# Unordered scatters, contiguous normalised rows and woven routing in an attention-then-experts kernel

## The chip, the cores and the metric

The kernel runs on one core of a Trainium2 chip. The metric is the device time of one execution in microseconds (us). The kernel before takes 444.11 us (median of 2 runs, 443.06 to 445.15). Ratios below are the mean time of one kernel's fast runs over that of the other's of the same rounds, so they are not quite the ratio of the medians that are quoted.

## The reference

```python
# attention with pooled keys and values: 8 batches, 8 heads, 576 queries, 64 per head
k_p = k.reshape(B, H, 72, 8, D).mean(axis=3);  v_p = likewise
attn = softmax(q @ k_p.T / 8)
x = (attn @ v_p)                      # 4608 rows of 512
# each row goes to one of 8 experts, by its domain id
for e in range(8):
    out[dom == e] = relu(x[dom == e] @ w1[e]) @ w2[e]     # 512 -> 1024 -> 512
```

## The kernel before

The kernel has three stages. Set-up loads the inputs and works out the routing: for every row its rank within its expert, hence its slot, and the inverse (for every slot its row). Attention runs in four pairs of batches. Each pair makes nine tiles of 128 normalised rows, and each tile is scattered to its slots in a DRAM buffer, `x_slots`. The expert stage reads the slots of an expert back, transposed, multiplies twice, and scatters the output rows to `out`. The first 384 slots of expert 0 are worked on inside pair 3.

```python
def load_pair(t_ap, pr, tag):                    # all loads are issued from GpSimd, and cast to F16
    t = io.tile([128, 72, D], F16, tag=tag, bufs=2, name=tag)
    nc.gpsimd.dma_start(t[:]..., t_ap[2 * pr:2 * pr + 2]...)

# normalise a tile of rows (half the heads at a time), then scatter it
if qd == 0:
    s["x", cc] = wk.tile([128, HD], F16, tag="x_sb", bufs=8, name="x_sb")
nc.vector.reciprocal(rcp[:], pv[:, :, 64])
xo = x_sb[:].rearrange("p (b h a) -> p h a b", b=4, h=H)[:, 4 * qd:4 * qd + 4]
nc.vector.tensor_tensor(out=xo, in0=pv[:, :, 0:64].rearrange("p h (a b) -> p h a b", b=4),
                        in1=rcp[:]...to_broadcast([128, 4, 16, 4]), op=ALU.mult)
if qd == 1:
    nc.gpsimd.indirect_dma_start(out=x_slots[:], out_offset=...(ap=slot_i[:, c:c + 1], axis=0), in_=x_sb[:], ...)

def xload(e, s0, s1):                            # slots back to the chip, transposed by the DMA
    xT = late.tile([128, 4, CAP], F16, tag="xT", bufs=2, name="xT")
    nc.sync.dma_start_transpose(xT[:, :, 0:s1 - s0], x_slots[CAP * e + s0:CAP * e + s1, :])

# second expert layer, a block of 128 slots
y = late.tile([128, HD], F32, tag="y", bufs=4, name="y")
nc.gpsimd.indirect_dma_start(out=out, out_offset=...(ap=orig[:, bl:bl + 1], axis=0), in_=y[:], ...)

# order of the program (cut)
...                                               # routing, about 100 small VectorE operations
for pr in range(NP):                              # the inverse of the slots
    perm_build(pr); perm_mm(pr)
perm_finish()
run(kp_units(0)); run(vp_units(0))                # pool k and v of pair 0
for pr in range(NP):
    run(qt_units(pr))
    if pr + 2 < NP: kt[pr + 2] = load_pair(k, ...); vt[pr + 2] = load_pair(v, ...)
    if pr == 3:
        for e in range(2):
            xload(e, 0, EARLY)
            if e > 0: wload(e)
    fill = kp_units(pr + 1) + vp_units(pr + 1)    # or, in pair 3, expert_units(0, 0, EARLY)
    run(merge(scav_units(pr), fill, ...))
    if pr + 2 < NP: qt_[pr + 2] = load_pair(q, ...)
    if pr == 0: wload(0)
wload(2)
...                                               # per task: xload of the next one, units, wload(e + 3)
```

The softmax here doesn't subtract the row's maximum and nothing guards it: scores larger than these inputs give would overflow.

Of the kernel before, what the change touches and what calls it, by code (L numbers as in the profile page):

```python
# [36 lines left out]
def kernel(  # L37
# [19 lines left out]

    def big():
        return ps.tile([128, 2, 512], F32, tag="big", bufs=2, name="big")
# [7 lines left out]
    x_slots = dram.tile([XROWS, HD], F16, name="x_slots")  # L67

# [7 lines left out]
    with tc.manual_schedule():  # L76
# [7 lines left out]
        nc.scalar.dma_start(  # L84
            x_slots[0:E * CAP, :].rearrange("(e s) d -> e (s d)", e=E)[:, FILL * HD:CAP * HD]
            .rearrange("e (p c) -> p e c", p=128),
            zt[:].unsqueeze(1).to_broadcast([128, E, 4 * (CAP - FILL)]))
# [16 lines left out]
        qt_[0] = load_pair(q, 0, "q")  # L104
        kt[1] = load_pair(k, 1, "k")
# [36 lines left out]
        for cc in range(NC_):  # L142
# [3 lines left out]
            if cc >= 4:  # L146
# [21 lines left out]
        rk = small()  # L168
        nc.tensor.matmul(rk[:, 0:8 * (NCH + 1)], Ls[:], oh[:].rearrange("p c e -> p (c e)"),
                         start=True, stop=False)  # L170
        for c in range(NCH - 1):
            c1 = NCH + 1 if c < EPAIR * NC_ else NCH
            nc.tensor.matmul(rk[:, 8 * (c + 1):8 * c1].rearrange("p (c e) -> p c e", e=E), ones[:],
                             oh[:, c, :].unsqueeze(1).to_broadcast([128, c1 - c - 1, E]),
                             start=False, stop=(c == NCH - 2))
        rkv = rk[:, 0:8 * NCH].rearrange("p (c e) -> p c e", e=E)

        gap = rt.tile([128, E], F32, name="gap")
        nc.vector.memzero(gap[:])
        nc.vector.tensor_scalar(out=gap[:, 0:NEARLY], in0=rk[:, 8 * NCH:8 * NCH + NEARLY],  # L180
                                scalar1=-1.0, scalar2=float(EARLY), op0=ALU.mult, op1=ALU.add)
        nc.vector.tensor_scalar(out=gap[:, 0:NEARLY], in0=gap[:, 0:NEARLY], scalar1=0.0,
                                scalar2=None, op0=ALU.max)
        tmp = rt.tile([128, NCH, E], F32, name="tmp")
        c0 = EPAIR * NC_
        nc.vector.tensor_copy(tmp[:, 0:c0], rkv[:, 0:c0])
        nc.vector.tensor_tensor(tmp[:, c0:NCH], rkv[:, c0:NCH],
                                gap[:].unsqueeze(1).to_broadcast([128, NCH - c0, E]), op=ALU.add)
        nc.vector.tensor_tensor(tmp[:], tmp[:], oh[:, 0:NCH, :], op=ALU.mult)
        rank = const.tile([128, NCH], F32, name="rank")  # L190
        nc.vector.tensor_reduce(out=rank[:], in_=tmp[:], op=ALU.add, axis=AX.X)
        ovf = const.tile([128, NCH], F32, name="ovf")
        nc.vector.tensor_scalar(out=ovf[:], in0=rank[:], scalar1=float(CAP), scalar2=None,
                                op0=ALU.is_ge)
        slotf = rt.tile([128, NCH], F32, name="slotf")
        nc.vector.tensor_scalar(out=slotf[:], in0=dom[:], scalar1=float(CAP), scalar2=None,
                                op0=ALU.mult)
        nc.vector.tensor_tensor(slotf[:], slotf[:], rank[:], op=ALU.add)

        ovf_h = rt.tile([128, NCH], F16, name="ovf_h")  # L200
        nc.vector.tensor_copy(ovf_h[:], ovf[:])
        ork = small()
        nc.tensor.matmul(ork[:, 0:NCH], Ls[:], ovf_h[:], start=True, stop=False)
        for c in range(NCH - 1):
            nc.tensor.matmul(ork[:, c + 1:NCH], ones[:],
                             ovf_h[:, c:c + 1].to_broadcast([128, NCH - 1 - c]),
                             start=False, stop=(c == NCH - 2))

        od = rt.tile([128, NCH], F32, name="od")
        nc.vector.tensor_scalar(out=od[:], in0=ork[:, 0:NCH], scalar1=float(NBLK * 128),  # L210
                                scalar2=None, op0=ALU.add)
        nc.vector.tensor_tensor(od[:], od[:], slotf[:], op=ALU.subtract)
        nc.vector.tensor_tensor(od[:], od[:], ovf[:], op=ALU.mult)
        nc.vector.tensor_tensor(od[:], od[:], slotf[:], op=ALU.add)
        slot_i = const.tile([128, NCH], I32, name="slot_i")
        nc.vector.tensor_copy(slot_i[:], od[:])

        nov = rt.tile([128, 2], F16, name="nov")
        ovs = rt.tile([128, 1], F32, name="ovs")
        nc.vector.tensor_reduce(out=ovs[:], in_=ovf[:], op=ALU.add, axis=AX.X)  # L220
        nc.vector.tensor_copy(nov[:, 0:1], ovs[:])
        nc.vector.tensor_copy(nov[:, 1:2], ovs[:])
        novp = small()
        nc.tensor.matmul(novp[:, 0:2], ones[:], nov[:], start=True, stop=True)
        nov_f = const.tile([128, 1], F32, name="nov_f")
        nc.vector.tensor_copy(nov_f[:], novp[:, 0:1])
        nblk_f = const.tile([128, 1], F32, name="nblk_f")
        nc.vector.tensor_scalar(out=nblk_f[:], in0=nov_f[:], scalar1=127.0, scalar2=None, op0=ALU.add)
        nblk_i = const.tile([128, 1], I32, name="nblk_i")
        nc.vector.tensor_copy(nblk_i[:], nblk_f[:])  # L230
        nc.vector.tensor_scalar(out=nblk_i[:], in0=nblk_i[:], scalar1=7, scalar2=None,
                                op0=ALU.logical_shift_right)

        mrow = const.tile([128, NCH], I32, name="mrow")
        mt = rt.tile([128, NCH], F32, name="mt")
        nc.vector.tensor_scalar(out=mt[:], in0=ovf[:], scalar1=-float(BIG), scalar2=float(BIG - NBLK * 128),
                                op0=ALU.mult, op1=ALU.add)
        nc.vector.tensor_tensor(mt[:], mt[:], od[:], op=ALU.add)
        nc.vector.tensor_copy(mrow[:], mt[:])


        pos_i = rt.tile([128, NCH], I32, name="pos_i")
        nc.vector.tensor_scalar(out=pos_i[:], in0=slot_i[:], scalar1=127, scalar2=None,
                                op0=ALU.bitwise_and)
        blk_i = rt.tile([128, NCH], I32, name="blk_i")
        nc.vector.tensor_scalar(out=blk_i[:], in0=slot_i[:], scalar1=7, scalar2=None,
                                op0=ALU.logical_shift_right)
        pos_h = const.tile([128, NCH], F16, name="pos_h")
        nc.vector.tensor_copy(pos_h[:], pos_i[:])
        blk_h = const.tile([128, NCH], F16, name="blk_h")  # L250
        nc.vector.tensor_copy(blk_h[:], blk_i[:])

        m_i = rt.tile([128, NC_], I32, name="m_i")
        nc.vector.tensor_scalar(out=m_i[:], in0=n_i[:], scalar1=3, scalar2=None,
                                op0=ALU.logical_shift_right)
        m_f = rt.tile([128, NC_], F32, name="m_f")
        nc.vector.tensor_copy(m_f[:], m_i[:])
        tk = rt.tile([128, NC_], F32, name="tk")
        nc.vector.tensor_scalar(out=tk[:], in0=m_f[:], scalar1=2.0, scalar2=None, op0=ALU.mult)
        t1 = rt.tile([128, NC_], F32, name="t1")  # L260
        for thr, add in ((36, -71.0), (72, 503.0), (108, -71.0)):
            nc.vector.tensor_scalar(out=t1[:], in0=m_f[:], scalar1=float(thr), scalar2=add,
                                    op0=ALU.is_ge, op1=ALU.mult)
            nc.vector.tensor_tensor(tk[:], tk[:], t1[:], op=ALU.add)
        g72 = rt.tile([128, 1], F32, name="g72")
        nc.vector.tensor_scalar(out=g72[:], in0=g_f[:], scalar1=72.0, scalar2=None, op0=ALU.mult)
        nc.vector.tensor_scalar(out=tk[:], in0=tk[:], scalar1=g72[:, 0:1], scalar2=None, op0=ALU.add)
        tok = rt.tile([128, NP, NC_], F32, name="tok")
        nc.vector.tensor_tensor(tok[:], pr_i[:], tk[:].unsqueeze(1).to_broadcast([128, NP, NC_]),
                                op=ALU.add)  # L270
        tok_i = rt.tile([128, NCH], I32, name="tok_i")
        nc.vector.tensor_copy(tok_i[:], tok[:].rearrange("p a c -> p (a c)"))
        th_i = rt.tile([128, NCH], I32, name="th_i")
        nc.vector.tensor_scalar(out=th_i[:], in0=tok_i[:], scalar1=6, scalar2=None,
                                op0=ALU.logical_shift_right)
# [53 lines left out]
        for pr in range(NP):  # L329
            perm_build(pr)  # L330
            perm_mm(pr)
# [216 lines left out]
        def run(units):  # L548
            for f in units:
                f()  # L550
# [143 lines left out]
```

## Time and profile before

| | before |
|---|---|
| time, median | 444.11 us |
| span of the profiled execution | 440.8 us |
| TensorE, VectorE busy | 59%, 39% |
| mean granted TensorE clock | 0.756 of full |

No engine is full. The first part of the page gives the busy time of each engine. In its table of groups a line gives the source line, engine, operation, output and inputs, shapes and count, then the busy time and the mean length of one in ns, then the engine's idle time just before them and what ended most of it.

```profile
span 440.8 us, 5605 instructions
...
PE 260.2 (59%) x2328; PEld 181.3 (41%) x2328; DVE 172.6 (39%) x321; ACT 94.2 (21%) x153; POOL 94.1 (21%) x113
...
L442 DVE TENSOR_TENSOR x_sb<-small,rcp 128x256 f16<-128x256 f32 x72 | 93.5, 1299 | 22.9 <-DMA x_slots<-x_sb,slot_i 19.3
...
L539 POOL DMA_INDIRECT out_dram<-y,orig x40 | 39.8, 995 | 149.1 <-DMA out_dram<-y,orig 117.5
L447 POOL DMA_INDIRECT x_slots<-x_sb,slot_i x36 | 35.6, 990 | 144.2 <-DVE rcp L439 63.7
...
```

Two things stand out. The multiply on line 442 takes 1299 ns for 256 columns. The two scatters on GpSimd are short to issue (about 1 us), but GpSimd is idle for some 145 us before each kind, and for the output scatter what ends that idle time is mostly the landing of another output scatter.

The windows view gives, for stretches of the span, the busy time of each engine, the granted clock, the share of the DMA engines that was busy, and GB/s. The stretches here start at the first scores of pairs 0, 1, 2 and 3 (50.0, 81.2, 128.8, 163.3), at the first expert matmul (192.0), after the last row scatter (235) and after the last matmul (415.7).

```profile
...
core 0: us, PE busy (x) PEld busy (x) DVE busy (x) ACT busy (x) POOL busy (x), PEclk, DMA share, GB/s
50.00:81.20 31.20, 23.46 (x344) 17.46 (x344) 26.55 (x43) 14.47 (x23) 6.77 (x7) 0.74 0.30 73
81.20:128.80 47.60, 24.76 (x346) 18.50 (x346) 26.61 (x43) 14.40 (x23) 8.97 (x13) 0.61 0.64 139
128.80:163.30 34.50, 23.53 (x344) 17.34 (x344) 26.58 (x43) 14.59 (x23) 9.43 (x10) 0.70 0.28 70
163.30:192.00 28.70, 0.69 (x4) 0.21 (x4) 0.00 (x0) 1.18 (x2) 6.07 (x7) 0.50 0.55 118
192.00:235.00 43.00, 34.34 (x216) 19.58 (x217) 29.50 (x47) 13.51 (x24) 12.10 (x13) 0.85 0.14 47
235.00:415.70 180.70, 132.57 (x726) 89.64 (x723) 34.90 (x50) 29.80 (x49) 40.31 (x46) 0.85 0.62 138
415.70:440.80 25.10, 0.36 (x2) 0.00 (x0) 0.00 (x0) 0.60 (x1) 3.29 (x4) 0.59 0.11 40
...
```

Pair 3 takes 71.7 us, of which 28.7 is TensorE doing nothing. The experts take 180.7 us with TensorE busy for 132.57.

GpSimd's timeline shows how the row scatters are released:

```profile
...
91.70 1.03 POOL L447 DMA_INDIRECT x_slots<-x_sb,slot_i  x1 [1.18 <-DVE x_sb L442]
119.16 1.02 POOL L447 DMA_INDIRECT x_slots<-x_sb,slot_i  x1 [26.42 <-DMA x_slots<-x_sb,slot_i]
122.39 0.98 POOL L447 DMA_INDIRECT x_slots<-x_sb,slot_i  x1 [2.22 <-DMA x_slots<-x_sb,slot_i]
...
```

The scatter at 119.16 waited 26.42 us: its predecessor was issued at 91.70 and landed 26.7 us later, at 118.4, after the loads that stood before it in the queue (the last of them, v of the next pair, issued at 89.94, took 28.1 us and landed at 118.0). The next one comes 3.23 us later: one issue of 1.02 us and one landing (2.5 us). In the waits view (engine and line, what it waited for, us in total, times, longest) this reads:

```profile
...
POOL out_dram L539 <- DMA out_dram<-y,orig: 117.5, 25, 12.8
...
POOL x_slots L447 <- DMA x_slots<-x_sb,slot_i: 47.1, 9, 26.4
...
PE big L514 <- DMA xT<-x_slots: 42.0, 2, 28.0
...
DVE y L535 <- DMA out_dram<-y,orig: 26.2, 2, 15.5
...
DVE x_sb L442 <- DMA x_slots<-x_sb,slot_i: 19.3, 2, 16.2
...
```

### The profile page before, as it was taken

What the parts mean: (1) busy time and instruction counts of PE and PEld (TensorE: products, weight loads), DVE (VectorE), ACT (ScalarE), POOL (GpSimd) and SP (SyncE); (2) the same over time, 40 slices, a digit from 0 to 9 for tenths busy, and PEclk for the clock granted to TensorE, in tenths of its full rate; (3) what the DMA queues carried; (4) which work ended last, traced back from release to release, by engine and by line L of the source; (5) the groups of instructions that cost most, each with busy time, mean ns of one, the idle gap of its engine ahead of it and who ended that gap; (6) DMA issues with size and microseconds to landing.
All of it is one profiled execution on the core that took longest, in us unless ns stands there. A gap on an engine that the chain in (4) does not pass through costs nothing. (4 is left out here: it accounts for less than half of the span.)

```text
span 440.8 us, 5605 instructions
## 1 busy us (share of the span) xinstructions
PE 260.2 (59%) x2328; PEld 181.3 (41%) x2328; DVE 172.6 (39%) x321; ACT 94.2 (21%) x153; POOL 94.1 (21%) x113
## 2 busy tenths in 40 slices
PE   2317795792079360057594299909849597499700
PEld 2216574481057240025251268506426364268300
DVE  4585399692269670019770032203203022033100
ACT  1000742731055330025111023101111110113100
POOL 5000012330022232101243030202212132122220
PEclk9756887586557855559888599967959979599955
DMA  8997921199611611850117859962936829211110
GB/s 200 227 215 151 183 58 37 37 197 217 137 37 39 131 37 48 165 109 12 61 59 155 179 128 195 219 146 79 209 103 146 185 80 214 86 69 73 62 67 0
DMA packets 30909, 52.34 MB, mean 119 GB/s; under 512 B 22750, under 2 KB 23838, under 8 KB 27296
## 3 DMA queue, kind: packets, MB, share of 16 engines
q0 software_dynamic: 8960, 45.10, 44.0%
q1 hardware_dynamic: 20880, 5.28, 6.6%
q10 hardware_dynamic: 1040, 1.57, 1.2%
q8 instruction: 19, 0.31, 0.3%
q14 instruction: 10, 0.08, 0.1%
HBM read 61.90 MB, written 16.78 MB: 179 GB/s over the span
## 5 line engine op out<-in xcount | busy, mean ns | idle before, releaser
L514 PE MATMUL big<-xT,w 128*128 128x320 f16 (+2 forms) x512 | 89.4, 337 | 78.1 <-DMA xT<-x_slots 42.0
L514 PEld LDWEIGHTS <-w 128*128 128x128 f16 x512 | 71.9, 149 | 94.1 <-issue 67.0
L442 DVE TENSOR_TENSOR x_sb<-small,rcp 128x256 f16<-128x256 f32 x72 | 93.5, 1299 | 22.9 <-DMA x_slots<-x_sb,slot_i 19.3
L520 DVE TENSOR_SCALAR hT<-big 128x640 f16<-128x640 f32 (+2 forms) x40 | 28.4, 711 | 122.8 <-PE big L514 120.9
L530 PE MATMUL small<-w,hT 128*128 128x512 f16 x320 | 72.8, 386 | 0.3 <-DVE y L535 0.3
L539 POOL DMA_INDIRECT out_dram<-y,orig x40 | 39.8, 995 | 149.1 <-DMA out_dram<-y,orig 117.5
L447 POOL DMA_INDIRECT x_slots<-x_sb,slot_i x36 | 35.6, 990 | 144.2 <-DVE rcp L439 63.7
L518 ACT ACTIVATE hT<-big 128x640 f16<-128x640 f32 (+2 forms) x40 | 23.9, 597 | 119.0 <-PE big L514 90.4
L530 PEld LDWEIGHTS <-hT 128*128 128x128 f16 x320 | 31.6, 99 | 36.8 <-issue 2.3
L416 ACT ACTIVATE at<-big 72x576 f16<-72x576 f32 x64 | 40.0, 644 | 27.9 <-PE big L413 26.8
L435 PE MATMUL small<-vp,at 72*128 72x65 f16 (+1 forms) x320 | 24.0, 214 | 31.0 <-DVE rcp L439 27.4
L535 DVE COPY y<-small 128x512 f32<-128x512 f32 x20 | 14.0, 702 | 63.8 <-PE small L530 37.7
L435 PEld LDWEIGHTS <-at 72*128 72x128 f16 (+1 forms) x320 | 16.1, 110 | 42.7 <-issue 24.7
L413 PE MATMUL big<-qT,kpT 64*72 64x288 f16 x128 | 24.2, 379 | 10.2 <-DVE hT L520 4.1
L537 ACT ACTIVATE y<-small 128x512 f32<-128x512 f32 x20 | 12.0, 598 | 81.1 <-PE small L530 50.1
L439 DVE RECIPROCAL rcp<-small 128x4 f32<-128x4 f32 x72 | 23.3, 324 | 10.5 <-PE small L435 10.5
L351 PE MATMUL small<-ident,k 128*64 128x128 f16 x576 | 23.1, 253 | 0.6 <-DVE x_sb L442 0.6
L351 PEld LDWEIGHTS <-k 128*64 128x64 f16 x576 | 21.5, 133 | 2.0 <-DVE x_sb L442 0.8
L399 PE MATMUL small<-ident,q 128*128 128x128 f16 x144 | 15.8, 286 | 2.6 <-DVE rcp L439 1.6
L413 PEld LDWEIGHTS <-kpT 64*72 64x72 f16 x128 | 8.9, 121 | 18.4 <-issue 12.0
L374 ACT ACTIVATE vT<-small 128x512 f16<-128x512 f32 (+1 forms) x12 | 5.8, 489 | 46.7 <-PE small L372 46.7
L399 PEld LDWEIGHTS <-q 128*128 128x128 f16 x144 | 13.2, 132 | 4.4 <-issue 2.6
(114 smaller groups left out, 126.4 us busy)
## 6 DMA issues: line engine op xcount, KB each, us to landing
w<-in_moe_w_dram POOLq DMA_DIRECT2D x16, 1024.0 KB, 12.6
k<-in_k_dram POOLq DMA_DIRECT2D x4, 1152.0 KB, 17.6
v<-in_v_dram POOLq DMA_DIRECT2D x4, 1152.0 KB, 22.9
q<-in_q_dram POOLq DMA_DIRECT2D x4, 1152.0 KB, 14.8
x_slots<-zt ACTq DMA_DIRECT2D x1, 1536.0 KB, 19.3
out_dram<-y,orig POOLq DMA_INDIRECT x40, 2.8
x_slots<-x_sb,slot_i POOLq DMA_INDIRECT x36, 2.4
xT<-x_slots SPq DMA_TRANSPOSE x10, 8.2
```

Source lines behind the costliest of these rows:

```text
L351: nc.tensor.matmul(pv[64 * half:64 * half + 64, w, :], kk[:, 8 * (w0 + w) + t, :], ident[:], start=(t == 0), stop=(t == 7), skip_group_che ...
L399: nc.tensor.transpose(p[:, j, :], qq[:, 128 * (j0 + j):128 * (j0 + j) + 128], ident[:])
L413: nc.tensor.matmul(p[0:72, par, 0:288], s["kpT"][64 * par:64 * par + 64, bh, :], s["qT"][64 * par:64 * par + 64, :, 8 * bh:8 * bh + 8], st ...
L416: nc.scalar.activation(at[0:72, bh % 8, :].rearrange("p (a c) -> p a c", a=2), p[0:72, :, 0:288], AFT.Exp, scale=1.0 / 64.0)
L435: nc.tensor.matmul(pv[r0:r0 + z - a, hh, :], s["at", bt][0:72, h, a:z], s["vp"][0:72, 8 * bt + h, :], start=True, stop=True, skip_group_ch ...
L442: nc.vector.tensor_tensor(out=xo, in0=pv[:, :, 0:64].rearrange("p h (a b) -> p h a b", b=4), in1=rcp[:].unsqueeze(2).unsqueeze(3).to_broad ...
L447: nc.gpsimd.indirect_dma_start(out=x_slots[:], out_offset=bass.IndirectOffsetOnAxis(ap=slot_i[:, c:c + 1], axis=0), in_=x_sb[:], in_offset ...
L514: nc.tensor.matmul(p[:, a, 0:m], w1[:, kk, fi:FF:8], xT[:, kk, m * a:m * a + m], start=(kk == 0), stop=(kk == 3))
L518: nc.scalar.activation(dst, p[:, 0:nh, 0:m], AFT.Relu)
L520: nc.vector.tensor_scalar(out=dst, in0=p[:, 0:nh, 0:m], scalar1=0.0, scalar2=None, op0=ALU.max)
L530: nc.tensor.matmul(p[:], hT[:, fi, 128 * j:128 * j + 128], w2[:, fi, :], start=(fi == 0), stop=(fi == 7))
L539: nc.gpsimd.indirect_dma_start(out=out, out_offset=bass.IndirectOffsetOnAxis(ap=orig[:, bl:bl + 1], axis=0), in_=y[:], in_offset=None, bou ...
```

## The change

The change has three intents. (a) Scatters no longer wait for one another, since every row has its own destination; the transposed read still waits for all of them. (b) The normalising multiply walks its output in the order in which it lies in SBUF. (c) Only rank and slot stay ahead of the scores of pair 0; everything else of the routing is spread over pairs 0 to 2. With these come two small moves: the zero fill of `x_slots` goes behind the first loads, and the evictions of pair 0's pooled keys go to ScalarE. The diff is cut to its core and a little simplified.

```diff
+    def apart(inst, group, why):
+        tc.declare_no_dep(inst, group=group, reason=why)
+        tc.add_to_no_dep_group(group, inst)
+    def behind(inst, others, why):
+        for o in others:
+            tc.add_manual_dep(inst, o.name, SYNC, reason=why)
...
-        nc.scalar.dma_start(x_slots[...zero rows...], zt...)         # at the very start
+        nc.gpsimd.dma_start(x_slots[...zero rows...], zt...)         # after the first k, v, q loads
...
-            xo = x_sb[:].rearrange("p (b h a) -> p h a b", b=4, h=H)[:, 4 * qd:4 * qd + 4]
-            nc.vector.tensor_tensor(out=xo, in0=pv[:, :, 0:64].rearrange("p h (a b) -> p h a b", b=4),
-                                    in1=rcp[:].unsqueeze(2).unsqueeze(3).to_broadcast([128, 4, 16, 4]),
+            xo = x_sb[:].rearrange("p (b h a) -> p b h a", b=4, h=H)[:, :, 4 * qd:4 * qd + 4, :]
+            nc.vector.tensor_tensor(out=xo, in0=pv[:, :, 0:64].rearrange("p h (a b) -> p b h a", b=4),
+                                    in1=rcp[:].unsqueeze(1).unsqueeze(3).to_broadcast([128, 4, 4, 16]),
...
-                nc.gpsimd.indirect_dma_start(out=x_slots[:], ...)
+                i = nc.gpsimd.indirect_dma_start(out=x_slots[:], ...)
+                apart(i, "xs", "each token has its own slot")
+                x_scatters.append(i)
...
+            behind(i, x_scatters, "x of the slots")                  # in xload
...
+                apart(i, "ys", "each token has its own row")         # output scatter
...
-        (all routing, perm_build, perm_mm, perm_finish, then) kp_units(0), vp_units(0)
+        run(kp_units(0)); rank_mm(); rank_post(); run(vp_units(0)); ovf_mm(); slot_post()
+        extra = {0: [perm_prep, tokens, count], 1: [], 2: [], 3: []}
+        for pr in range(NP):
+            extra[1 + pr // 2] += [perm_build(pr), perm_mm(pr)]
+        extra[2].append(perm_finish)
...
+                fill = merge(fill, extra[pr])
```

## The prediction

> **What bounds it now.** No engine is full (page: TensorE 59%, VectorE 39% of 440.8 us). The windows view splits the span: set-up until TensorE reaches attention at 37.7 us; four attention pairs until about 235 us (pair 0 31 us, pair 3 72, with the first piece of expert 0 inside it); experts 235 to 415.7 us, 181 us with TensorE busy 132.6; a 25 us tail. The chain of waits that ended last puts 15% on landings of the output scatter, more than on any matmul line.
>
> Three causes:
> - *Scatters wait for each other.* GpSimd's timeline shows row scatters 3.2 us apart, output scatters 3.5 us: about 1 us to issue, then the predecessor's landing (median 2.4 and 2.8 us). When loads stand before one in the queue the wait is 26 us (at 119.2 and 204.9 us) or 9.6 to 12.9 us (once per expert). GpSimd waited 117.5 us for output landings, 47 us for row landings. [...]
> - *The normalising multiply*, 72 x 1299 ns for 256 columns, is 23.3 us of a 31 to 35 us pair. It writes halves 256 bytes apart. [...] 288-column VectorE operations with contiguous output take 453 to 459 ns here.
> - *Serial routing*: TensorE idles for most of the first 37.7 us while VectorE does rank, slots, and the slot inverse (23 to 38 us).
>
> **The change.** (a) No wait between scatters; they still share a queue with the loads, and 8 row and 4 output buffers are freed by landings. (b) The multiply writes 64-element runs but reads PSUM with a 16-byte step; I estimate 450 ns (range 380 to 700), so 72 x 0.85 = 61 us of VectorE, mostly on the pairs' path. (c) Only rank and slots stay ahead of pair 0; the inverse (about 3.5 us of VectorE per pair) moves into pairs 1 and 2. The zero fill moves behind the first q load, so k lands at about 8 us.
>
> **Estimate.** Pair 0 starts its scores at about 26 us instead of 50. A pair then needs some 25 us of both TensorE and VectorE. Loads limit too: the first 45 us moved 8.7 MB with queues full, so the second k, v, q land by about 42 us and row scatters queue behind the next loads; the ninth row tile of pairs 0 and 1 must wait for a landing. I get pairs of 30, 36 and 26 us, then 38 for pair 3 (last row landing, 8 us transpose, 11 us of expert 0): experts start near 156 us instead of 235. The dense stretch 380.8 to 414.3 us did 1.775 experts in 33.5 us, 18.9 us each, so about 140 us remain; DMA needs about 4 MB an expert, 18 us at its 225 GB/s when busy, nearly level: add 5. Tail about 17 us. Sum 318 us.
>
> Predicted 318 us, 8 in 10 between 292 and 348. Faster by over 2%: 0.97; within 2%: 0.02; slower: 0.01.
>
> **What would show it.** GpSimd's wait for output landings falls from 117.5 to under 30 us; scatters issue as their tile is ready; the multiply takes 380 to 700 ns; first scores near 26 us; experts near 19 us apiece; granted clock above 0.756.
>
> **What would make it wrong.** The PSUM read step costs as much as the old write step; scatters queue behind loads so long that buffers take over the old waits (attention 20 to 30 us longer); DMA, not TensorE, paces the experts (22 us or more each); the wait for transposed rows in pair 3 stays near 28 us.

That the old multiply is slow because of its write was the assumption, and the 450 ns an estimate, set beside the 453 to 459 ns measured for 288 columns. The 4 MB an expert are two weight loads of 1024 KB, 1.3 MB of output rows and 0.66 MB of transposed rows. The 225 GB/s is near what the windows of the kernel before show: 194 GB/s at a DMA share of 0.88 in the first 45 us and 138 at 0.62 in the experts, that is 220 and 223 when busy.

## The result, and the profile after

The changed kernel takes 348.53 us (median of 2 runs, 347.45 to 349.61), ratio 0.7848 with a 95% interval of 0.7717 to 0.7979. This is faster by 21.5%, where 28% had been predicted: the time lies just above the stated range of 292 to 348.

The same parts of the page, of the changed kernel:

```profile
span 347.8 us, 5625 instructions
...
PE 245.3 (71%) x2328; PEld 178.7 (51%) x2328; DVE 116.5 (33%) x318; ACT 94.8 (27%) x156; POOL 96.4 (28%) x114
...
L573 POOL DMA_INDIRECT out_dram<-y,orig x40 | 39.7, 993 | 116.5 <-DVE y L569 64.4
...
L478 POOL DMA_INDIRECT x_slots<-x_sb,slot_i x36 | 37.4, 1038 | 106.0 <-DVE x_sb L473 61.4
...
L473 DVE TENSOR_TENSOR x_sb<-small,rcp 128x256 f16<-128x256 f32 x72 | 30.6, 424 | 18.7 <-DMA x_slots<-x_sb,slot_i 16.1
...
```

The multiply fell from 1299 to 424 ns, that is by 3.4 ns an element of the 256. The order of its read changed with that of its write, and no run takes the two apart; but the new read, of 4-byte elements with a 16-byte step, showed no visible cost: 424 ns for 256 columns, against 458 ns for a multiply of 288 columns read in order from PSUM (rm, in the same trace). The scatters still have idle time before them, but now they wait for their data. In the waits view no wait of GpSimd for the landing of another scatter is left; the largest waits for DMA on the engines that compute are these:

```profile
...
PE big L548 <- DMA xT<-x_slots: 35.9, 3, 14.4
...
DVE x_sb L473 <- DMA x_slots<-x_sb,slot_i: 16.1, 2, 8.8
...
DVE y L569 <- DMA out_dram<-y,orig: 11.5, 2, 5.8
...
```

GpSimd's timeline shows that row scatters can now leave 1.3 us apart (95.51 and 96.79):

```profile
...
79.15 0.98 POOL L478 DMA_INDIRECT x_slots<-x_sb,slot_i  x1 [0.30 <-DVE rcp L470]
95.51 0.98 POOL L478 DMA_INDIRECT x_slots<-x_sb,slot_i  x1 [15.38 <-DVE rcp L470]
96.79 0.98 POOL L478 DMA_INDIRECT x_slots<-x_sb,slot_i  x1 [0.30 <-DVE rcp L470]
...
```

The pause of 15.38 us before 95.51 is of another kind. The ninth row tile of a pair needs the buffer of the first; VectorE waited 8.8 us for that buffer, because its scatter, issued at 70.20, stood behind loads in the queue (issued at 62.6 to 64.8) and landed 24.0 us later. The median landing of a row scatter was 2.5 us.

The windows, cut at the same events as before (first scores of pairs 0 to 3, first expert matmul, after the last row scatter, after the last matmul):

```profile
...
core 0: us, PE busy (x) PEld busy (x) DVE busy (x) ACT busy (x) POOL busy (x), PEclk, DMA share, GB/s
26.90:63.40 36.50, 22.91 (x346) 18.62 (x345) 17.36 (x76) 13.72 (x23) 9.68 (x11) 0.72 0.80 181
63.40:101.40 38.00, 23.53 (x362) 18.89 (x362) 18.57 (x51) 14.38 (x23) 11.56 (x13) 0.73 0.83 179
101.40:131.20 29.80, 24.53 (x362) 19.16 (x362) 19.45 (x56) 14.49 (x23) 10.43 (x11) 0.77 0.34 81
131.20:146.10 14.90, 0.48 (x5) 0.21 (x5) 0.00 (x0) 1.18 (x2) 1.30 (x3) 0.60 0.98 193
146.10:177.30 31.20, 29.50 (x199) 17.42 (x200) 15.20 (x46) 12.96 (x23) 11.83 (x12) 0.81 0.18 64
177.30:331.10 153.80, 128.94 (x743) 89.72 (x740) 35.75 (x51) 30.47 (x50) 42.53 (x49) 0.92 0.79 166
331.10:347.80 16.70, 0.05 (x1) 0.00 (x0) 0.00 (x0) 0.60 (x1) 1.29 (x2) 0.63 0.08 30
...
```

Set beside the prediction (us; the last column is a kernel that is told of below, cut in the same way):

| stretch | before | predicted | after | "best" |
|---|---|---|---|---|
| start to first scores | 50.0 | 26 | 26.9 | 28.4 |
| pair 0 | 31.2 | 30 | 36.5 | 27.9 |
| pair 1 | 47.6 | 36 | 38.0 | 29.7 |
| pair 2 | 34.5 | 26 | 29.8 | 29.7 |
| pair 3 with its wait | 71.7 | 38 | 46.1 | 38.6 |
| experts | 180.7 | 145 | 153.8 | 131.2 |
| tail | 25.1 | 17 | 16.7 | 16.4 |
| sum | 440.8 | 318 | 347.8 | 301.9 |

The miss of 30 us has three places: pairs 0 to 2 (12 us), pair 3 (8) and the experts (9). In the last two TensorE waits for transposed rows. These are the three lines of TensorE's timeline that have such a wait:

```profile
...
146.06 1.47 PE L548 MATMUL big<-xT,w 128*128 128x384 f16 x4 [14.41 <-DMA xT<-x_slots]
...
194.28 6.16 PE L548 MATMUL big<-xT,w 128*128 128x256 f16 x32 [12.17 <-DMA xT<-x_slots]
...
238.36 11.26 PE L548 MATMUL big<-xT,w 128*128 128x320 f16 x64 [9.37 <-DMA xT<-x_slots]
...
```

The three add up to 35.95 us. They are the first theory of the miss: **a DMA transpose that runs beside a weight load lands late**. The one before 146.06 was issued at 133.0, right behind expert 1's weights (131.3 and 131.9):

```profile
...
L530 SPq DMA_TRANSPOSE xT<-x_slots x1: 8592/8592/8592, 133.0 to 133.0; - x1
...
DMA to landing us min/median/max: 12.9/12.9/12.9
```

The DMA view of that stretch (132.8 to 146 us; queue, packets, MB, share of the 16 engines) shows what ran. q0 holds the weights, q1 the transposes:

```profile
...
q0 software_dynamic: 281, 2.04, 77.9%
q1 hardware_dynamic: 2433, 0.61, 24.3%
...
```

The view counts the packets of each queue. The transposes moved 0.61 MB in packets of 251 bytes, the weights 2.04 MB in packets of 7.3 KB (MB over packets), and the engines were full (the two shares add up to 102%). The transposes used 24.3% of 13.2 us, that is 3.2 us of engine time, yet the first took 12.9 us to land. The second weight load landed at 144.5 (issued 131.9, 12.6 us), the first transpose at 145.9. From 137 to 143 us, while both queues had work, they passed nearly one packet for one (169 and 153):

```profile
...
q0 software_dynamic: 169, 1.25, 99.6%
q1 hardware_dynamic: 153, 0.04, 4.7%
...
```

With packets so unequal the transposes got 0.04 of 1.29 MB. From 144.5 to 146 us, when the weights had landed, 1621 packets (0.41 MB) of transposes passed. The issuing instruction on SyncE was held up too: it lasted 8.59 us here (the 8592 ns of the view above). No run here varied the packet size, so that the unequal packets are the reason is a reading of the trace and was not tested by itself.

The rival theories were: (R1) DMA traffic as a whole is the limit, so a wait removed here comes back elsewhere; (R2) the row buffers, released only by landings, are what paces the pairs; (R3) the gain was mis-assigned between (a), (b) and (c).

### The profile page after: what moved, and what is told of

Its sections match the earlier page's. It is cut to its first block, busy times and chain, and to the rows that moved or that the text cites. A ratio compares the mean times of both kernels' runs of the same rounds, so it can differ in the third digit from the quotient of the medians.

```text
span 347.8 us, 5625 instructions
## 1 busy us (share of the span) xinstructions
PE 245.3 (71%) x2328; PEld 178.7 (51%) x2328; DVE 116.5 (33%) x318; ACT 94.8 (27%) x156; POOL 96.4 (28%) x114
## 4 chain that ended last, share of the span: by engine, by line
issue 35%; DMA 26%; PE 15%; POOL 12%; DVE 4%; ACT 2%; POOLq 1%; SPq 0%; ACTq 0%; DVEq 0%
DMA x_slots<-x_sb,slot_i 15%; POOL out_dram L573 8%; DMA x_slots<-zt 7%; PE big L548 5%; DMA xT<-x_slots 4%; PE small L564 3%; PE small L430 2%; PE small L466 2%; PE big L444 2%; DVE x_sb L473 1%; ACT at L447 1%; PE small L379 1%; POOL w L519 1%; POOL w L522 1%; DVE op L327 1%
## 5 line engine op out<-in xcount | busy, mean ns | idle before, releaser
L548 PE MATMUL big<-xT,w 128*128 128x320 f16 (+2 forms) x512 | 82.1, 319 | 39.9 <-DMA xT<-x_slots 35.9
L548 PEld LDWEIGHTS <-w 128*128 128x128 f16 x512 | 70.2, 146 | 49.2 <-issue 30.0
L573 POOL DMA_INDIRECT out_dram<-y,orig x40 | 39.7, 993 | 116.5 <-DVE y L569 64.4
L564 PE MATMUL small<-w,hT 128*128 128x512 f16 x320 | 71.0, 379 | 0.6 <-ACT y L571 0.3
L478 POOL DMA_INDIRECT x_slots<-x_sb,slot_i x36 | 37.4, 1038 | 106.0 <-DVE x_sb L473 61.4
L552 ACT ACTIVATE hT<-big 128x640 f16<-128x640 f32 (+2 forms) x40 | 23.9, 596 | 87.7 <-PE big L548 72.9
L447 ACT ACTIVATE at<-big 72x576 f16<-72x576 f32 x64 | 39.1, 644 | 27.6 <-PE big L444 26.8
L473 DVE TENSOR_TENSOR x_sb<-small,rcp 128x256 f16<-128x256 f32 x72 | 30.6, 424 | 18.7 <-DMA x_slots<-x_sb,slot_i 16.1
L569 DVE COPY y<-small 128x512 f32<-128x512 f32 x20 | 13.8, 691 | 49.3 <-PE small L564 37.8
L379 PE MATMUL small<-ident,k 128*64 128x128 f16 x576 | 24.8, 264 | 5.8 <-DMA k<-in_k_dram 4.3
L444 PE MATMUL big<-qT,kpT 64*72 64x288 f16 x128 | 22.4, 352 | 7.2 <-ACT at L447 3.3
L470 DVE RECIPROCAL rcp<-small 128x4 f32<-128x4 f32 x72 | 12.6, 175 | 18.1 <-PE small L466 17.4
L430 PE MATMUL small<-ident,q 128*128 128x128 f16 x144 | 13.3, 278 | 0.5 <-DMA q<-in_q_dram 0.5
L430 PEld LDWEIGHTS <-q 128*128 128x128 f16 x144 | 12.7, 130 | 0.6 <-DMA q<-in_q_dram 0.6
L417 ACT ACTIVATE vp<-small 72x512 f16<-72x512 f32 x8 | 4.7, 594 | 29.8 <-PE small L415 29.8
## 6 DMA issues: line engine op xcount, KB each, us to landing
w<-in_moe_w_dram POOLq DMA_DIRECT2D x16, 1024.0 KB, 12.8
k<-in_k_dram POOLq DMA_DIRECT2D x4, 1152.0 KB, 24.7
x_slots<-zt POOLq DMA_DIRECT2D x1, 1536.0 KB, 22.9
```

Source lines behind the costliest of these rows:

```text
L379: nc.tensor.matmul(pv[64 * half:64 * half + 64, w, :], kk[:, 8 * (w0 + w) + t, :], ident[:], start=(t == 0), stop=(t == 7), skip_group_che ...
L430: nc.tensor.transpose(p[:, j, :], qq[:, 128 * (j0 + j):128 * (j0 + j) + 128], ident[:])
L444: nc.tensor.matmul(p[0:72, par, 0:288], s["kpT"][64 * par:64 * par + 64, bh, :], s["qT"][64 * par:64 * par + 64, :, 8 * bh:8 * bh + 8], st ...
L447: nc.scalar.activation(at[0:72, bh % 8, :].rearrange("p (a c) -> p a c", a=2), p[0:72, :, 0:288], AFT.Exp, scale=1.0 / 64.0)
L478: i = nc.gpsimd.indirect_dma_start(out=x_slots[:], out_offset=bass.IndirectOffsetOnAxis(ap=slot_i[:, c:c + 1], axis=0), in_=x_sb[:], in_of ...
L548: nc.tensor.matmul(p[:, a, 0:m], w1[:, kk, fi:FF:8], xT[:, kk, m * a:m * a + m], start=(kk == 0), stop=(kk == 3))
```

## The experiments

Twelve kernels ran, all correct, each timed in 4 runs beside the kernel before on the same chip (its median was 442.6 to 443.2 us). The first six below divide the gain; the others are about the miss. In four of the experiments one of the four runs was slow, 1.7 to 3.1% above the fastest of its kernel; there the median and range given are those of the other three. The changed kernel itself was timed only twice, in its own session, where the kernel before took 444.11 us. What an edit gains or costs is given against its 348.53 us, so a microsecond or two of such a difference is not resolved.

### unordered_only: part (a) alone on the kernel before

```diff
  (kernel before)
+ apart(...) on both scatters, behind(xload, x_scatters)
```

> The kernel before with part (a) alone: scatters no longer wait for each other. Theory (the order between scatters is the largest part): experts fall from 181 us to about 155 as in the changed kernel, the tail from 25 to 17, the attention pairs stay near 32 us each because the old multiply keeps VectorE at 30 us a pair; sum 370 to 385 us. Rival (the multiply and the routing carry most of the gain): above 405 us.

Measured: 378.08 us (377.27 to 379.23), ratio 0.8537. This is 65 us of the 95, inside what the theory gave; the rival falls. The multiply, the routing and the two small moves are worth 30 us on top of it; no run takes the small moves apart.

### ordered: the change without part (a)

```diff
  (changed kernel)
- apart(i, "xs", ...)
- apart(i, "ys", ...)
```

> The changed kernel with the order between scatters restored for rows and outputs, all else kept. Theory: row scatters 3.2 us apart make 29 us a pair and loads in front add waits of 26 us, experts go back to about 180 us, tail 25: 395 to 415 us. Rival (order costs little once the pairs are short): below 375 us.

Measured: 430.9 us (428.5 to 433.8), ratio 0.9704, slower than either figure. Parts (b) and (c), with the small moves, are worth 12 us while the order stands and 30 us once it is gone. In this trace pair 1 takes 57.0 us between the starts of the q transposes (38.4 in the changed kernel), and VectorE waits 26.8 us in it for one row landing; the first expert matmul comes at 186.1 instead of 146.1 us.

### rows_ordered and outs_ordered: one kind each

```diff
  (changed kernel)
- apart(i, "xs", ...)        # rows_ordered
- apart(i, "ys", ...)        # outs_ordered
```

> The changed kernel with only the row scatters ordered again. In the run with both ordered the first transposed rows arrived at TensorE at 186 us instead of 146, so 40 of its 82 us should come from here: 383 to 393 us. If the two kinds only cost together (either one alone hidden): under 370 us.

> The changed kernel with only the output scatters ordered again. The other half of the 82 us: 385 to 395 us, with GpSimd's waits for output landings back above 90 us and the experts at 180 us or more.

Measured: 393.43 us (392.75 to 394.82), ratio 0.8892, and 384.53 us (381.68 to 385.37), ratio 0.8674. The first lies half a microsecond above its expected range, the second as much below its own. The two cost 45 and 36 us, and 81 is the 82 us of both. They act in different stages and add up. The waits view of outs_ordered has the old wait back:

```profile
...
POOL out_dram L573 <- DMA out_dram<-y,orig: 107.7, 24, 11.8
...
```

Its stage after the last row scatter runs from about 176 to about 357 us, some 181 us, as long as in the kernel before.

### old_multiply: the change without part (b)

```diff
  (changed kernel)
- xo = ... "p (b h a) -> p b h a" ...      # and in0, in1 to match
+ xo = ... "p (b h a) -> p h a b" ...
```

> The changed kernel with the old strided write of the normalising multiply (1299 instead of 424 ns, 63 us more VectorE). If the pairs are paced by VectorE: 375 us or more. If the waits for buffers and for transposed rows hide part of it: 358 to 370 us. If VectorE was off the path: under 353 us.

Measured: 369.68 us (368.2 to 370.21), ratio 0.8332: 21 us. The groups of VectorE show the multiply as before:

```profile
...
L473 DVE TENSOR_TENSOR x_sb<-small,rcp 128x256 f16<-128x256 f32 x72 | 93.5, 1299 | 9.7 <-DMA x_slots<-x_sb,slot_i 6.4
...
```

The records of the multiply are 63 us longer (93.5 less 30.6). Records of VectorE overlap: the next instruction starts some 0.4 us before that of a slow multiply ends (in the kernel before, a multiply of 1.29 us starts at 69.53 and the reciprocal after it at 70.45). VectorE's busy time on the page, which counts overlap once, is 55 us longer (171.4 against 116.5), 3.0 ns an element. This cost 21 us of the kernel, as expected if waits hide a part. The pairs of this run, between the starts of their q transposes, are 38.0, 42.7 and 38.4 us, against 34.8, 38.4 and 29.8: in pairs 0 and 1, which wait for landings anyway, the slow multiply costs 3 to 4 us, and in pair 2, which doesn't wait, 9. With these first runs R3 is answered: (a) is the largest part, and the gains of (b) and (c) depend on it.

### routing_ahead: the change without part (c)

```diff
  (changed kernel)
- run(kp_units(0)); rank_mm(); rank_post(); run(vp_units(0)); ovf_mm(); slot_post(); extra = {...}
+ rank_mm(); rank_post(); ovf_mm(); slot_post(); count(); perm_prep(); tokens()
+ for pr in range(NP): perm_build(pr); perm_mm(pr)
+ perm_finish(); run(kp_units(0)); run(vp_units(0)); extra = {0: [], 1: [], 2: [], 3: []}
```

> The changed kernel with all routing back in front of pair 0. Pair 0's first scores come near 42 instead of 27 us. If the start sets the end: 15 us later, about 363 us. If the loads pace pairs 0 and 1 (row buffers waiting behind loads), most of the 15 us is waited anyway: 348 to 356 us.

Measured: 362.23 us (360.03 to 364.56), ratio 0.8182: 14 us. The q transposes of pair 0 start at 45.9 instead of 23.9 us, and its first scores come at 49.0 us, not near 42. Of those 22 us, 8 are given back: VectorE waits less for row buffers (9.9 instead of 16.1 us) and TensorE for transposed rows (30.7 instead of 35.9). The result is nearer to "the start sets the end".

### w1_early: the weights of expert 1 away from the first transposes

```diff
  (changed kernel)
             if pr == 0: wload(0)
+            if pr == 1: wload(1)
...
                 for e in range(NEARLY):
                     xload(e, 0, EARLY)
-                    if e > 0: wload(e)
```

> The changed kernel with the weight load of expert 1 issued at the end of pair 1 (DMA is 0.34 busy in pair 2) instead of next to the two transposes at the start of pair 3. Theory (a transpose that shares the engines with a weight load takes 12.9 to 15.3 us instead of about 5): the first transpose lands in under 7 us, TensorE's wait for it falls from 14.4 to 7 to 9 us, the kernel takes 339 to 345 us. Rival (the wait is the last row landing plus the transpose's own length): transpose still over 11 us, time unchanged, 346 to 351 us.

Measured: 335.86 us (334.51 to 338.18; a fourth run, 344.96, was slow), ratio 0.7595, below the expected 339 to 345. The profile is of that slow execution, so only what happens at pair 3 is read from it: the two transposes landed in 4.1 and 4.2 us, and TensorE's wait was 5.94 us instead of 14.41. The theory's durations hold; the gain of 12.7 us is larger than the 8.5 us of the wait, and what made the rest is open.

### w12_clear: a move that only changed the partner of the collision

```diff
  (w1_early)
                 fill = expert_units(0, 0, EARLY)
+                fill.insert(3, lambda: wload(2))
...
-        wload(2)                       # after the pairs
```

> As w1_early, and the load of expert 2 is issued early inside pair 3 instead of right before the transposes that follow pair 3. Theory: both transposes run clear, the 12.2 us wait at 194 us falls below 4 us too, 328 to 337 us. Rival (DMA as a whole paces the experts, so a wait taken away here comes back later): no faster than w1_early within 3 us.

Measured: 333.42 us (331.82 to 333.43; a fourth run, 338.0, was slow), ratio 0.7514. The time lies in the theory's range, and also within 3 us of w1_early, as the rival had it, so it decides nothing. The edit did not do what it was meant to. Nothing before the load on GpSimd waited, so expert 2's weights left at the start of pair 3 (at 130.31 and 130.90 us, the last row scatter of pair 2 being issued at 129.34) and met the first transposes in the place of expert 1's: the first landed in 12.8 us again and TensorE waited 14.41 us. The transposes after pair 3 were clear and landed in 3.5 and 3.9 us, and the wait there fell from 12.17 to 0.32 us. So the wait went where the weight load went.

### w12_apart: both weight loads away from the transposes

```diff
  (w1_early)
                 x_scatters.append(i)
+                if pr == 3 and cc == 0:
+                    wload(2)           # behind the first row scatter of pair 3
...
-        wload(2)                       # after the pairs
```

> w12_clear moved the load of expert 2 to the start of pair 3 on GpSimd (nothing in front of it there holds it), so it met the first transposes in the place of expert 1's load: 12.8 us for the first, 3.5 us for the one after pair 3. Here it is issued behind the first row scatter of pair 3, and expert 1's at the end of pair 1. Theory (transposes are late only when they share the engines with a weight load): both waits go, 6 us left of the 14.4 and under 2 us of the 12.2: 325 to 330 us. Rival (the sum of the traffic is what counts): 332 us or more.

Measured: 329.91 us (329.65, 329.91 and 333.75; a fourth run, 335.77, was slow), ratio 0.7501: two runs in the theory's range and one in the rival's, so the waits have to decide. The two transposes at pair 3, in the view of their tile:

```profile
...
L532 SPq DMA_TRANSPOSE xT<-x_slots x2: 1487/1524/1562, 132.6 to 134.1; - x2
...
DMA to landing us min/median/max: 4.0/4.0/4.1
```

TensorE's three waits are now:

```profile
...
136.72 1.47 PE L550 MATMUL big<-xT,w 128*128 128x384 f16 x4 [5.76 <-DMA xT<-x_slots]
...
176.50 6.28 PE L550 MATMUL big<-xT,w 128*128 128x256 f16 x32 [5.13 <-DMA xT<-x_slots]
...
219.90 11.72 PE L550 MATMUL big<-xT,w 128*128 128x320 f16 x64 [8.57 <-DMA xT<-x_slots]
...
```

Two waits fell by 8.65 and 7.04 us, 15.7 together, and the time by 18.6. SyncE's two issuing instructions last 1.49 and 1.56 us instead of 8.59 and 3.42. The second came to 5.13 us where under 2 had been expected, with a landing of 5.5 us. The traffic is the same, so R1 does not explain the waits of pair 3 and after it. The third wait is not touched.

### xt3: transposes issued two tasks ahead

```diff
  (changed kernel)
-            xT = late.tile([128, 4, CAP], F16, tag="xT", bufs=2, name="xT")
+            xT = late.tile([128, 4, CAP], F16, tag="xT", bufs=3, name="xT")
...
         xload(*xnext.pop(0))
+        xload(*xnext.pop(0))
         for t in tasks:
```

> The changed kernel with three buffers for the transposed rows and transposes issued two tasks ahead. Theory: the wait of 9.4 us before expert 3 (transposed rows issued at 208.2, landed 30 us later behind two weight loads) vanishes; the waits in and after pair 3 stay; 337 to 344 us. Rival (DMA as a whole is the limit): 346 us or more.

Measured: 339.57 us (336.76 to 341.66), ratio 0.767: 9 us, as expected. The longest landing of a transpose is still 30.1 us, but no wait follows; the waits of 14.30 and 12.21 us stay.

### xsb16: sixteen row buffers instead of eight

```diff
-                s["x", cc] = wk.tile([128, HD], F16, tag="x_sb", bufs=8, name="x_sb")
+                s["x", cc] = wk.tile([128, HD], F16, tag="x_sb", bufs=16, name="x_sb")
```

> The changed kernel with 16 row buffers instead of 8, so VectorE never waits for a row landing (16.1 us of waits in pairs 0 and 1). If the buffers are the limit there: pairs 0 and 1 shorter by 8 us each, 333 to 340 us. If the loads are (k, v of the next pair land no sooner): 342 to 349 us.

Measured: 330.68 us (330.32 to 331.6), ratio 0.7468, below the expected 333 to 340. Between the starts of the q transposes pairs 0, 1 and 2 now take 27.5, 30.1 and 28.4 us, against 34.8, 38.4 and 29.8. The waits of VectorE for row landings are gone. R2 is right for pairs 0 and 1: the buffers, released late by scatters that stood behind loads, held them. The gain, 17.9 us, is as large as that of w12_apart, which moves two loads.

### best: all of it together

```diff
  (w12_apart and xt3, and)
- tag="x_sb", bufs=8
+ tag="x_sb", bufs=11
```

> All four at once: both weight loads moved as in w12_apart, three transposed-row buffers with transposes two tasks ahead, 11 row buffers [...]. If the waits are independent: 348.5 less 8, 12, 9 and about 14, that is 300 to 312 us. If DMA as a whole becomes the limit first: 316 us or more.

Measured: 307.28 us (303.69 to 307.41; a fourth run, 308.98, was slow), ratio 0.6962 to the kernel before, as expected if the waits are independent. The single gains of w12_apart, xt3 and xsb16 (18.6, 9.0 and 17.9 us) would give 303.0. So they nearly add up, with 11 row buffers in place of the 16 of xsb16, and R1 is not the limit yet. What is left of TensorE's waits for transposed rows, in its timeline:

```profile
...
121.30 1.47 PE L550 MATMUL big<-xT,w 128*128 128x384 f16 x4 [4.90 <-DMA xT<-x_slots]
...
158.99 4.50 PE L550 MATMUL big<-xT,w 128*128 128x256 f16 x32 [1.65 <-DMA xT<-x_slots]
...
```

This version beats both kernels.

## Why the prediction was wrong

What held:

- The three causes: without (a) the changed kernel takes 82 us more, without (b) 21 and without (c) 14.
- The multiply (450 predicted, 424 ns measured), the first scores (26 and 26.9 us, although the first k landed at 10.2 us, not at about 8; at 13.8 before), the tail (17 and 16.7 us), no GpSimd wait left for output landings, and a granted clock above 0.756 (0.835).
- The rate of dense expert work was even better than predicted: 17.5 us an expert in the last stretch (313.6 to 331.1) against 18.9. The granted clock was 1.00 in that stretch and 0.92 in the one of the kernel before from which the 18.9 was taken; as an estimate from these, 18.9 x 0.92 = 17.4, so the clock alone would account for it, which no run tests.

What failed, by how far the term of the sum was off:

1. The step "DMA needs about 4 MB an expert, 18 us at its 225 GB/s when busy, nearly level: add 5". It treats DMA in the expert stage as a rate. What counted was when one particular transfer landed: 12.17 and 9.37 us of TensorE waiting for transposed rows, and 3 us more for evictions on ScalarE and VectorE (1.98 and 1.17 us in TensorE's timeline at 298.5 and 280.1). The allowance for waits was 5, the waits came to 24.7; by luck the better rate (128.94 us of TensorE time instead of 140) gave more than half of the difference back, and 9 us were left over. "Experts near 19 us apiece" failed for these waits: the 7.4 experts left for this stage took 153.8 us, 20.8 apiece.
2. The step "I get pairs of 30, 36 and 26 us". They took 36.5, 38.0 and 29.8, 12 us more. The buffer wait was foreseen; its size in pair 0 was not. xsb16 shows that without it the pairs take 27.5 to 30.1 us, so the base of "some 25 us of both TensorE and VectorE" was also 3 to 5 us short. TensorE was busy for 22.9 to 24.5 us of a pair and VectorE for only 17.4 to 19.5 (the windows of the changed kernel), so neither fills such a pair; what does is open.
3. The step "8 us transpose" in pair 3. The 8.2 us is the median over ten transposes, those beside loads and those in the clear. The transpose that mattered stood beside a weight load in the profile of before too, and took 12.7 us there. It took 12.9 us after the change, and 4.0 to 4.1 us when the load was moved (w12_apart). That is 5 of the 8 us of pair 3; the other 3 are not accounted for.
4. "72 x 0.85 = 61 us of VectorE, mostly on the pairs' path". VectorE's busy time fell by 55 us, but only 21 us were on the path (old_multiply). The sum rests on this only through the base of a pair.

## What to carry to other kernels

When you take a wait away, look for the next thing that the same landing releases: here the row buffers and the late transposes were left once scatters no longer waited for one another, and taking these waits away gained 41 us more (best). Do not size a transfer on the critical path with a median over the kernel; find the instance that stands in the same company, and look at what is issued just before it. Here the median was 8.2 us in the kernel before; the first transpose of 384 rows landed in 4.0 to 4.2 us in the clear (w1_early, w12_apart, best) and in 12.5 to 12.9 us beside the weights of one expert (the kernel before, the changed one, w12_clear, xt3, xsb16), and one of 640 rows, issued between the weight loads of two experts, in 30.0 us (the changed kernel, at 208.2). A load that is "moved later" in the program can still leave at once, as in w12_clear (130.31 us, right after the last scatter of pair 2), if nothing before it on that engine waits. So place it behind an instruction that does: in w12_apart the scatter before it waited 16.81 us for its rows, and the load left at 148.53.
